# First two tiles of a fused induced attention and feed-forward kernel: second attention with tokens on the partitions, blocks in turns of four, weight loads spread among those of x

## The chip, the cores and the metric

One core of a Trainium2 chip runs the whole kernel. TensorE multiplies (PE in the rows; PEld is its weight loads), VectorE (DVE), ScalarE (ACT) and GpSimd (POOL) do the elementwise work, SyncE (SP) issues nearly all transfers. The metric is the device time of one execution in microseconds; lower is better.

## The reference

x is [4, 12480, 128] (4 batches of 12480 tokens), `inducing` is [32, 128], w_in [128, 2048], w_out [2048, 128]. The two weights come as 64-bit floats; everything else and the output are 32-bit.

```
def mab(q, kv):
    s = scale * (q @ kv.transpose(0, 2, 1))
    s = s - s.max(-1, keepdims=True)
    a = np.exp(s)
    a /= a.sum(-1, keepdims=True) + 1e-09
    return a @ kv
h = mab(I, x)            # first attention: 32 queries over 12480 tokens, per batch
y = mab(x, h)            # second attention: every token over the 32 rows of h
g = y @ w_in; g = np.maximum(0.01 * g, g)
out = g @ w_out
```

## The kernel before, in words

The second attention's weights A (32 per token) are never multiplied with h alone: h @ w_in is formed once per batch (`hws`, 2048 columns), so the feed-forward's first product is A @ (h @ w_in). The slope of 0.01 is taken out: the relu part carries 0.99, and a linear part A @ (h @ (0.01 w_in @ w_out)) is added at the end (`w12` is 0.01 w_in @ w_out, `m2s` is h @ w12). Values that feed the fast matmuls are split into a rounded part and a rest (hi and lo): A's halves lie stacked in four blocks of 32 partitions (hi, lo, hi, lo: tile `A4`), `hws` likewise, and w_out is `w_hi` and `w_lo`.

Tokens are taken in tiles of 512 columns; six groups of 2048 tokens (four tiles each) and a rest of 192 make up a batch. A tile is 16 slots, one per block of 128 columns of w_in. In slot u, `ffn_first` (L745) does one matmul into `ph` (L750), a relu on ScalarE into `ghi` (L758) and the rest on VectorE into `glo` (L760), three slots ahead; `ffn_second` (L770) does three matmuls into `po` (L778), and at a tile's last slot one more with `m2s` (L784). `store` transposes `po` on VectorE (L794) and writes it out. `ph` has three buffers, so the fourth first-product waits for the first `glo`.

All engines get their work in the order in which the program emits it; nothing is reordered but TensorE's weight loads. The main loop (L875 to L904) emits per slot the two feed-forward parts and then one step of each of several generators: conversions (`late`), weights, stores, stacking, second attentions, the next batch's first attention. A step marked HEAVY puts up a `debt` of 3, which holds back the other debt-bound generators for three slots.

Ahead of the loop is the ramp for batch 0. `first_batch` (L465) issues 25 transfers of x, with the four w_in chunks (512 KB each, one per 512 columns) behind the transfers named in LOADS (L69, counted from 0), and then works group by group: transposes of x on TensorE (L499), ScalarE copies (L502), scores against `inducing` (L268), running maximum and exponential (L280 to L329), sums h (L388). ROUNDS and DRAIN (L73, L77) say which background steps go between these: "l" is a quarter of the conversion of a weight chunk (`from_double`, L110: L123 and L124; L128; L132; L136 and two GpSimd steps L139, L140), "t" a turn of one w_in chunk by four transposes (L213). Five rounds convert one chunk each; the last round and the drain before hT (`normalise`, L452) convert the rest but one. w_out's chunks are split into `w_hi` (ScalarE, L188) and `w_lo` (GpSimd, L189), each one chunk behind its conversion.

Then, from hT on, RAMP (L78) interleaves `expand_weights` (hT @ w_in, four products L576, each split by ScalarE L555 and VectorE L557) with the second attention of group 0 (`second`, L624) on VectorE: scores L268, transpose L639, maximum L642, subtract L644, exponential L650, sum L654 to L656, multiply L658, transpose L667. `stack_first` (L708) spreads tile 0's A over the partitions with a matmul (L713), ScalarE (L716) and two VectorE steps (L719); tiles 1 to 3 of group 0 go by `stack` (L671) with 4 transfers each. The other groups' second attentions run in the loop with their two tensor steps on GpSimd (L644, L658 with POOL as engine). The w12 product (four groups of four matmuls, L225) is begun in the ramp and ended in the loop.

## Time and profile before

| what | us |
|---|---|
| median of 3 runs | 1626.44 (1625.77 to 1627.32) |
| the profiled execution | 1626.58 |
| its span | 1624.8 |
| TensorE busy | 1600.9 (99%) |
| VectorE busy | 1291.0 (79%) |
| ScalarE busy | 1008.7 (62%) |
| GpSimd busy | 109.4 (7%) |
| first feed-forward matmul starts | 62.32 |
| HBM read, written | 48.94 MB, 25.56 MB |

The span is what the trace covers, from the first instruction to the last; the execution's own time is 1.8 us longer. Busy is the time in which an engine ran an instruction. Matmuls are pipelined, so a busy TensorE is one that always has a next matmul. The rows below give durations of single instructions, what an engine waited for in square brackets, and the granted clock of TensorE (PEclk, 1.00 for 2.4 GHz and 0.50 for 1.2 GHz).

### The profile page before, as it was taken

The numbers are of one execution on the slowest core, as the hardware profiler recorded it, in microseconds if no ns is written. First come the engines' busy times: TensorE is split into PE (matmuls) and PEld (weight loads), VectorE is DVE, ScalarE is ACT, GpSimd is POOL, SyncE is SP. The second block draws the span as 40 slices with busy tenths as digits, with TensorE's granted clock in tenths as the row PEclk, the third lists the DMA queues.
The fourth block names the chain that finished last, engine by engine and source line by source line (L and its number), as shares of the span: only waits on it lengthen the run. The fifth ranks groups of instructions, "written<-read, shape, count | busy, mean of one in ns | idle before, by whom it ended". The sixth has DMA issues, their size and how long they took to land.

```text
span 1624.8 us, 22382 instructions
## 1 busy us (share of the span) xinstructions
PE 1600.9 (99%) x7881; PEld 1257.6 (77%) x7881; DVE 1291.0 (79%) x2228; ACT 1008.7 (62%) x1767; POOL 109.4 (7%) x108
## 2 busy tenths in 40 slices
PE   7799999999999999999999999999999999999998
PEld 5577777777778777777777777777777788888886
DVE  6788888787888887877787888877878777777776
ACT  5466666666666665666666666656666666666665
POOL 3310000000001000000010000000001000000000
PEclk9899999999999999999999999999999999999999
DMA  7323323522224344522123434532212111212211
GB/s 262 74 56 53 69 64 70 114 64 58 46 43 95 50 96 95 101 65 53 33 46 74 80 70 102 104 68 50 59 25 40 34 31 39 41 25 41 42 23 20
DMA packets 401503, 104.44 MB, mean 64 GB/s; under 512 B 372432, under 2 KB 374896, under 8 KB 401392
## 3 DMA queue, kind: packets, MB, share of 16 engines
q1 hardware_dynamic: 401344, 103.01, 31.3%
q8 instruction: 62, 1.02, 0.3%
q14 instruction: 49, 0.40, 0.1%
q10 hardware_dynamic: 48, 0.02, 0.0%
HBM read 48.94 MB, written 25.56 MB: 46 GB/s over the span
## 4 chain that ended last, share of the span: by engine, by line
PE 96%; DVE 2%; DMA 1%; ACT 0%; issue 0%; SPq 0%; DVEq 0%
PE po L778 67%; PE ph L750 23%; PE s_ps L268 3%; PE po L784 1%; PE h_ps L388 1%; DMA xr<-in_x_dram 1%; DVE cv_a L124 0%; PE xT_ps L499 0%; DVE cv_a L132 0%; PE mx_ps L297 0%; DVE glo L760 0%; DVE ay L416 0%; PE winT_ps L213 0%; ACT ghi L758 0%; PE w_ps L225 0%
## 5 line engine op out<-in xcount | busy, mean ns | idle before, releaser
L760 DVE SCALAR_TENSOR_TENSOR glo<-ph,ghi 128x512 fp32r<-128x512 f32 (+1 forms) x1568 | 1051.6, 681 | 303.9 <-ACT ghi L758 298.7
L758 ACT ACTIVATE ghi<-ph 128x512 fp32r<-128x512 f32 (+1 forms) x1568 | 933.6, 597 | 573.5 <-PE ph L750 571.8
L750 PE MATMUL ph<-A,hws 128*128 128x512 f32 (+1 forms) x1600 | 622.8, 393 | 3.1 <-DVE A L719 2.3
L778 PE MATMUL po<-ghi,w_hi 128*128 128x512 f32 (+1 forms) x1568 | 618.6, 395 | 0.0
L778 PE MATMUL po<-glo,w_hi 128*128 128x512 f32 (+1 forms) x1568 | 617.3, 394 | 0.0
L778 PE MATMUL po<-ghi,w_lo 128*128 128x512 f32 (+1 forms) x1568 | 613.8, 391 | 0.0
L750 PEld LDWEIGHTS ph<-A,hws 128*128 128x128 f32 x1600 | 300.7, 188 | 91.3 <-DVE glo L760 13.3
L778 PEld LDWEIGHTS po<-ghi,w_lo 128*128 128x128 f32 x1568 | 294.7, 188 | 70.1
L778 PEld LDWEIGHTS po<-glo,w_hi 128*128 128x128 f32 x1568 | 294.7, 188 | 66.5
L778 PEld LDWEIGHTS po<-ghi,w_hi 128*128 128x128 f32 x1568 | 294.8, 188 | 61.0
L689 POOL TENSOR_TENSOR alo<-aT,ahi 128x512 fp32r<-128x512 f32 x24 | 31.2, 1299 | 735.4 <-ACT ahi L684 590.5
L794 DVE STREAM_TRANSPOSE osb<-po 128x512 f32<-128x512 f32 (+1 forms) x98 | 68.9, 703 | 1.7 <-PE po L784 1.7
L644 POOL TENSOR_TENSOR y<-y,mx 128x512 f32<-128x512 f32 (+1 forms) x27 | 25.4, 940 | 419.9 <-DVE mx L642 419.9
L369 DVE STREAM_TRANSPOSE xT<-xc 128x512 f32<-128x512 f32 x72 | 50.5, 701 | 0.0
L658 POOL TENSOR_TENSOR y<-y,sm 128x512 f32<-128x512 f32 (+1 forms) x27 | 25.4, 939 | 212.9 <-DVE sm L656 130.2
L784 PE MATMUL po<-A,m2s 128*128 128x512 f32 (+1 forms) x100 | 38.6, 389 | 0.0
L388 PEld LDWEIGHTS h_ps<-xr,ay 128*32 128x32 f32 (+1 forms) x784 | 22.5, 112 | 12.6 <-issue 12.4
L268 PE MATMUL s_ps<-xT,indT 128*32 128x512 f32 x192 | 27.3, 642 | 1.6 <-ACT xT L502 1.6
L388 PE MATMUL h_ps<-xr,ay 128*32 128x128 f32 (+1 forms) x784 | 28.0, 280 | 0.0
L268 PE MATMUL s_ps<-xT,hT 128*32 128x512 f32 x192 | 25.6, 605 | 0.0
L280 DVE TENSOR_SCALAR_CACHE_REDUCE e<-s_ps 128x512 f32<-128x512 f32 (+1 forms) x28 | 17.1, 612 | 7.7 <-PE s_ps L268 7.2
L784 PEld LDWEIGHTS po<-A,m2s 128*128 128x128 f32 x100 | 18.7, 187 | 4.2
(98 smaller groups left out, 390.5 us busy)
## 6 DMA issues: line engine op xcount, KB each, us to landing
xr<-in_x_dram SPq DMA_DIRECT2D x96, 256.0 KB, 4.4
out_dram<-osb SPq DMA_DIRECT2D x384, 64.0 KB, 2.2
xc<-in_x_dram SPq DMA_DIRECT2D x288, 64.0 KB, 2.7
A<-ahi SPq DMA_DIRECT2D x190, 64.0 KB, 2.0
A<-alo SPq DMA_DIRECT2D x190, 64.0 KB, 2.0
raw<-in_moe_w_in_dram SPq DMA_DIRECT2D x4, 512.0 KB, 7.9
raw<-in_moe_w_out_dram SPq DMA_DIRECT2D x4, 512.0 KB, 6.6
hws<-hwhi SPq DMA_DIRECT2D x24, 64.0 KB, 2.0
```

Of the source, the lines that this page charges most:

```text
L268: nc.tensor.matmul(dst, lhsT, rhs, start=True, stop=True)
L369: nc.vector.transpose(t[:, j, :], blk.rearrange("p n c -> p (n c)"))
L388: nc.tensor.matmul(hp[32 * k : 32 * k + 32, :C], ay[:rows, 4 * q + k, :], xb[:rows, k, :], start=(q == 0), stop=(4 * q + 4 >= K), tile_pos ...
L644: eng.tensor_tensor(out=yv, in0=yv, in1=mx[:rows, :K].unsqueeze(2).broadcast_to([rows, K, M]), op=ALU.subtract,)
L658: eng.tensor_tensor(out=yv, in0=yv, in1=smv.unsqueeze(2).broadcast_to([rows, K, M]), op=ALU.mult)
L689: (eng or nc.gpsimd).tensor_tensor(out=alo[sl], in0=aT.pop((b, g))[: 32 * J, :], in1=ahi[sl].bitcast(F32), op=ALU.subtract,)
L750: nc.tensor.matmul(ph[:, o : o + w], hw[b][1][:, f * P : (f + 1) * P], A4[t][:, o : o + w], start=True, stop=True,)
L758: nc.scalar.activation(ghi[:, :n], ph[:, :n], AF.Relu)
L760: nc.vector.scalar_tensor_tensor(out=glo[:, :n], in0=ph[:, :n], scalar=0.0, in1=ghi[:, :n].bitcast(F32), op0=ALU.max, op1=ALU.subtract,)
L778: nc.tensor.matmul(po[:, :n], w[:, f, :], r[:, :n], start=(f == 0 and r is ghi and w is w_hi), stop=False)
L784: nc.tensor.matmul(po[:, o : o + w], hw[b][2], a4[:, o : o + w], start=False, stop=(o + w == n),)
L794: nc.vector.transpose(osb[:, :n], po[:, :n])
```

## The change

The x transfers that carry a weight chunk behind them are now the fifth, ninth, thirteenth, seventeenth and twenty-first (counted from 1), and the fifth chunk is w_out's first, in a buffer of its own. Two chunks of conversion (w_out's third and fourth) move into the loop, the second ends in the drain; the split of w_out is a generator of its own (`parts_of_w_out`), and w12 is summed chunk by chunk with a VectorE step each. Tiles 0 and 1 no longer go through `second` and the stacking: `quick` makes each tile's scores with the tokens on the partitions (x as the weights, hT's 32 columns as the moving operand), does maximum, exponential and sum along 32 columns on VectorE and ScalarE, and turns the result to the stacked layout by 16 matmuls with the identity. `stack_first` goes. Group 0's `second` now runs in the loop like the others, for tiles 2 and 3. Only the first of the four hT @ w_in products and its split are ahead of the loop. Slots of tiles 0 and 1 alternate in turns of four blocks (slots 0 to 3 tile 0, 4 to 7 tile 1, 8 to 11 tile 0, ...); from tile 2 on the order is as before. The values of batch 1 wait until weights and linear part of batch 0 are done.

```
-    LOADS = [3, 5, 7, 9]
+    LOADS = [4, 8, 12, 16, 20]
     ROUNDS = [
         [""] * 5, ["l", "l", "", "", "ll", "", ""], *[["l", "l", "", "", "ll", "", "", ""]] * 4,
-        ["ll", "ll", "", "", ""],
+        ["l", "", "l", "", ""],
     ]
-    DRAIN = ["", "", "llt", "t", "", "t", "", "", "tll"]
-    RAMP = ["wwm", "w", "w", "", "", "wl", "w", "", "", "w", "wll"]
+    DRAIN = ["", "", "s", "lt", "l", "", "t", "", ""]
+    QUICK = 2
+    TURN = 4
...
+        nc.vector.tensor_tensor(out=low_rows, in0=own[:, 1:2], in1=own[:, 3:4], op=ALU.add)
+        nc.vector.tensor_scalar(
+            out=signs, in0=low_rows, scalar1=2.0, scalar2=-1.0, op0=ALU.mult, op1=ALU.add
+        )
...
     def load_w_out(c):
-        raw = sb.tile([P, 4, P, 2], I32, tag="xc", name="raw", bufs=3)
+        tag, bufs = ("xc", 3) if c else ("hws", 2)
+        raw = sb.tile([P, 4, P, 2], I32, tag=tag, name="raw", bufs=bufs)
...
+    def parts_of_w_out():
+        for c in range(NF // 4):
+            while c >= len(ready):
+                yield
             if c:
-                split_w_out(c - 1)
-            yield
-        split_w_out(NF // 4 - 1)
-        yield
+                yield from idle(3)
+            split_w_out(c)
+            yield
...
     def setup_w12():
         for c in range(NF // 4):
-            while c == len(wraws) or (late and c == len(wraws) - 1):
+            while c >= len(ready):
                 yield
+            if c == len(ready) - 1:
+                yield from idle(3)
+            acc = aux_ps("w12_ps")
             for f in range(4):
                 nc.tensor.matmul(
-                    acc[:, :P], winTs[c][:, f, :], wraws[c][:, f, :],
-                    start=(c == 0 and f == 0), stop=(c == NF // 4 - 1 and f == 3),
+                    acc[:, :P], winTs[c][:, f, :], wraws[c][:, f, :], start=(f == 0), stop=(f == 3)
                 )
...
-                    xT[0, g] = sb.tile([P, K, J, 32], F32, tag="xT", name="xT", bufs=RING)
+                    shape = [P, K, J, 32] if g else [P, J, 32 * K]
+                    xT[0, g] = sb.tile(shape, F32, tag="xT", name="xT", bufs=RING)
...
         if b == 0:
...
             for c in range(4):
                 sl = slice(c * TOK, (c + 1) * TOK)
-                yield from split(hws[:, sl], pws[c], TOK, 1.0 - SLOPE)
+                pw = ps_s.tile([P, TOK], F32, tag="hp", name="hw_ps")
+                nc.tensor.matmul(pw, hT, w_in_sb[:, sl], start=True, stop=True)
                 yield
...
+                yield from split(hws[:, sl], pw, TOK, 1.0 - SLOPE)
+                yield
             return
...
+    def quick(t):
+        b, g, (j,) = tiles[t][0]
+        hT = hw[b][0]
+        sp = aux_ps("q_ps")
+        for c in range(4):
+            nc.tensor.matmul(
+                sp[:, c * M : (c + 1) * M], xT[b, g][:, j, c * P : (c + 1) * P], hT[:, :M],
+                start=True, stop=True,
+            )
+        yield
+        sv = sp[:, : 4 * M].rearrange("p (c m) -> p c m", m=M)
+        mx = sb.tile([P, 4], F32, tag="mx", name="qmx")
+        nc.vector.tensor_reduce(out=mx, in_=sv, op=ALU.max, axis=AX.X)
+        y = sb.tile([P, 4, M], F32, tag=("hwhi", "hwlo")[t], name="qy", bufs=1)
+        nc.vector.tensor_tensor(
+            out=y, in0=sv, in1=mx.unsqueeze(2).broadcast_to([P, 4, M]), op=ALU.subtract
+        )
+        nc.scalar.activation(y, y, AF.Exp, scale=SCALE)
+        yield
+        sm = sb.tile([P, 4], F32, tag="sm", name="qsm")
+        nc.vector.tensor_reduce(out=sm, in_=y, op=ALU.add, axis=AX.X)
+        nc.vector.tensor_scalar_add(sm, sm, 1e-9)
+        nc.vector.reciprocal(sm, sm)
+        nc.vector.tensor_tensor(
+            out=y, in0=y, in1=sm.unsqueeze(2).broadcast_to([P, 4, M]), op=ALU.mult
+        )
+        yield
+        pa = ps_o.tile([P, TOK], F32, tag="po", name="a4_ps")
+        for c in range(4):
+            for r in range(4):
+                nc.tensor.matmul(
+                    pa[32 * r : 32 * r + 32, c * P : (c + 1) * P], y[:, c, :], ident,
+                    start=True, stop=True, tile_position=(0, 32 * r),
+                )
+        yield
         A4[t] = a4 = sb.tile([P, TOK], F32R, tag="A4", name="A4", bufs=A4_BUFS)
...
+        nc.scalar.mul(a4, pa, signs)
+        yield
+        nc.vector.scalar_tensor_tensor(
+            out=a4, in0=pa, scalar=low_rows, in1=a4.bitcast(F32), op0=ALU.mult, op1=ALU.subtract
+        )
+        yield
...
+    slots = [
+        (t, f) for f0 in range(0, NF, TURN) for t in range(QUICK) for f in range(f0, f0 + TURN)
+    ]
+    slots += [(t, f) for t in range(QUICK, NT) for f in range(NF)]
...
+        one, two = [quick(0)], [quick(1)]
+        for lane in (
+            one, two, weights, one, two, turning, one, one, weights, one, two, two,
+            weights, one, two, two,
+        ):
+            step(lane)
+        stacks[0] = stacks[0][QUICK:]
         stacking = [stack(s) for s in stacks]
-        weights = [chain(*weights, *twelve, expand_linear(0))]
-        seconds = [second(0, g) for g in [1, 2, RG, 3, 4, 5]]
+        linear = [chain(*turning, *twelve, expand_linear(0))]
+        seconds = [second(0, g) for g in [0, 1, 2, RG, 3, 4, 5]]
...
             step(late)
+            step(splits)
             step(weights)
+            step(linear)
             if not debt[0]:
                 step(stores)
             step(stacking)
-            if not weights and not debt[0]:
+            if not debt[0]:
                 step(seconds)
...
-                if values:
+                if values and not ((linear or weights) and b == 0):
```

## Rows read from the trace of the kernel before

**Rows 1.** The chain of waits that ended last: its shares of the span by engine.
```profile
PE 96%; DVE 2%; DMA 1%; ACT 0%; issue 0%; SPq 0%; DVEq 0%
```
**Rows 2.** Busy time of each engine in four stretches: stretch, its length, busy us and instructions of each engine, granted clock, share of the transfer engines, GB/s.
```profile
0.00:62.30 62.30, 45.23 (x409) 29.61 (x410) 42.77 (x117) 31.37 (x66) 21.30 (x22) 0.94 0.58 183
62.30:68.60 6.30, 5.72 (x13) 4.09 (x14) 3.54 (x6) 4.19 (x8) 1.39 (x2) 0.53 0.69 117
68.60:101.00 32.40, 32.40 (x164) 26.11 (x163) 24.80 (x47) 19.39 (x35) 7.05 (x6) 1.00 0.33 76
101.00:1618.80 1517.80, 1517.58 (x7298) 1197.74 (x7296) 1219.18 (x2059) 953.79 (x1658) 79.64 (x79) 1.00 0.30 59
```
**Rows 3.** The chain of waits in order of time, pieces of the first two tiles: start us, us, what. L784 is a tile's last matmul; the one at 100.80 ends tile 1.
```profile
71.11 0.89 PE w_ps L225 x8
...
88.77 0.70 PE po L778 x3
89.47 0.23 PE ph L750
...
100.80 0.24 PE po L784
```
**Rows 4.** TensorE in order of time, the first groups of the first attention: transposes of x (L499) and scores (L268); in brackets what it waited for.
```profile
13.43 1.97 PE L499 MATMUL xT_ps<-ident,xr 128*128 128x128 f32 x8 [0.54 <-DMA xr<-in_x_dram]
...
16.07 1.93 PE L268 MATMUL s_ps<-xT,indT 128*32 128x512 f32 x8 [0.45 <-ACT xT L502]
...
22.06 1.04 PE L268 MATMUL s_ps<-xT,indT 128*32 128x512 f32 x8
23.04 1.97 PE L499 MATMUL xT_ps<-ident,xr 128*128 128x128 f32 x16
...
26.41 1.06 PE L268 MATMUL s_ps<-xT,indT 128*32 128x512 f32 x8 [0.28 <-ACT xT L502]
```
**Rows 5.** Busy time by stretch, 10 to 20 us; the columns are those of rows 2.
```profile
10.00:20.00 10.00, 9.01 (x44) 5.92 (x37) 5.30 (x16) 4.42 (x9) 2.55 (x2) 1.00 1.04 398
```
**Rows 6.** All engines in order of time, last round and drain: two conversion steps, the maximum's matmul, a w_in turn, the h product of group 5, the copy that makes hT.
```profile
39.98 0.68 DVE L132 SCALAR_TENSOR_TENSOR cv_a<-cv_a,cv_b 128x512 int32<-128x512 int32 x1
...
40.70 0.43 DVE L136 TENSOR_SCALAR cv_b<-cv_a 128x512 int32<-128x512 int32 x1
...
42.88 0.59 PE L297 MATMUL mx_ps<-rd,e 128*128 128x4 f32 x2 [2.87 <-DVE rd L292]
...
43.33 1.09 PE L213 MATMUL winT_ps<-ident,w_in_sb 128*128 128x128 f32 x4
...
44.35 1.94 PE L388 MATMUL h_ps<-xr,ay 128*32 128x128 f32 x32
...
50.30 0.27 ACT L461 COPY hT<-hT_ps 128x128 f32<-128x128 f32 x1 [0.58 <-PE hT_ps L459]
```
**Rows 7.** The same view between hT and the first feed-forward matmul.
```profile
53.23 1.79 DVE L644 TENSOR_TENSOR y<-y,mx 128x512 f32<-128x512 f32 x1
...
60.05 0.59 ACT L716 CAST A<-a_ps 128x512 fp32r<-128x512 f32 x1 [3.31 <-PE a_ps L713]
...
62.32 1.62 PE L750 MATMUL ph<-A,hws 128*128 128x512 f32 x3 [2.31 <-DVE A L719]
```
**Rows 8.** The same view, rows that serve as prices: a 128-column VectorE step out of PSUM, an h product at the upper clock level, two hT @ w_in products (four records).
```profile
22.49 0.28 DVE L402 COPY hacc<-h_ps 128x128 f32<-128x128 f32 x1
...
25.05 1.08 PE L388 MATMUL h_ps<-xr,ay 128*32 128x128 f32 x32
...
51.62 1.98 PE L576 MATMUL hw_ps<-w_in_sb,hT 128*128 128x512 f32 x4
```
**Rows 9.** The chain of waits, pieces of the first slots: start us, us, what.
```profile
63.75 0.70 DVE glo L760
...
66.57 0.43 PE ph L750
67.00 1.28 PE po L778 x3
```
**Rows 10.** Busy time by stretch of 2 us; the columns are those of rows 2, the granted clock is the third from the right.
```profile
40.00:42.00 2.00, 0.01 (x2) 0.00 (x0) 1.97 (x7) 1.51 (x4) 0.73 (x1) 0.74 0.03 4
...
46.00:48.00 2.00, 2.00 (x18) 1.71 (x10) 1.00 (x5) 0.59 (x1) 0.00 (x0) 0.56 0.06 8
...
60.00:62.00 2.00, 0.01 (x1) 0.00 (x0) 1.92 (x4) 0.59 (x1) 0.00 (x0) 0.86 0.18 28
```
**Rows 11.** All engines in order of time: conversion steps on VectorE with and without a GpSimd instruction under way, a ScalarE cast that waits for GpSimd, the attention's subtract on GpSimd.
```profile
38.04 1.27 POOL L140 TENSOR_TENSOR wraw<-cv_a,cv_t 128x512 f32<-128x512 f32 x1
...
38.37 1.22 DVE L124 TENSOR_SCALAR cv_a<-raw 128x512 f32<-128x512 f32 x1
...
44.09 1.50 DVE L128 TENSOR_SCALAR cv_b<-raw 128x512 int32<-128x512 int32 x1
...
55.78 0.43 DVE L124 TENSOR_SCALAR cv_a<-raw 128x512 f32<-128x512 f32 x1
...
69.83 0.62 ACT L188 CAST w_hi<-wraw 128x512 fp32r<-128x512 f32 x1 [1.89 <-POOL wraw L140]
...
86.86 1.05 POOL L644 TENSOR_TENSOR y<-y,mx 128x512 f32<-128x512 f32 x1 [13.31 <-DVE mx L642]
```
**Rows 12.** The tile that holds batch 1's to 3's rounded h @ w_in: instruction, count, durations in ns, first and last start in us.
```profile
L601 ACT ACTIVATE hwhi<-hw_ps x3: 592/592/592, 392.4 to 1129.4; 128x512 fp32r<-128x512 f32 x3
```

More of the change, by code (lines that the diff above doesn't have):

```diff
@@ L99, in induced_attention_then_leaky_ffn @@
     own = const.tile([P, 4], F32, tag="own", name="own")
+    low_rows = const.tile([P, 1], F32, tag="low_rows", name="low_rows")
+    signs = const.tile([P, 1], F32, tag="signs", name="signs")
     w_in_sb = const.tile([P, DFF], F32, tag="w_in_sb", name="w_in_sb")
@@ L263, in columns_product @@
         dst, rhs = ps[32 * j : 32 * j + 32, :w], xT[b, g]
-        if b == 0:
+        if b == 0 and g:
             dst, rhs = dst.rearrange("p (k r) -> p k r", r=32), rhs[:, :, j, :]
@@ L478, in first_batch @@
             if i in LOADS:
-                raws.append(load_w_in(LOADS.index(i)))
+                c = LOADS.index(i)
+                raws.append(load_w_in(c) if c < NF // 4 else load_w_out(0))
         chains, ays = {}, {}
@@ L501, in turn @@
                 )
+            t = xT[0, g]
+            if g == 0:
+                t = t.rearrange("p j (k r) -> p k j r", r=32)
             nc.scalar.copy(
-                xT[0, g][:, 4 * q : 4 * q + nk].rearrange("p k j r -> p (k j r)"),
-                pt[:, : nk * rows],
+                t[:, 4 * q : 4 * q + nk],
+                pt[:, : nk * rows].rearrange("p (k j r) -> p k j r", k=nk, r=32),
             )
@@ L567, in expand_weights @@
         if b == 0:
-            pws = []
-            def product():
-                c = len(pws)
-                if c == 1:
-                    pw = ps_s.tile([P, TOK], F32, tag="hp", name="hw_ps")
-                else:
-                    pw = aux_ps("hw_ps")
-                nc.tensor.matmul(
-                    pw, hT, w_in_sb[:, c * TOK : (c + 1) * TOK], start=True, stop=True
-                )
-                pws.append(pw)
-            for _ in range(3):
-                product()
-                yield
             for c in range(4):
                 sl = slice(c * TOK, (c + 1) * TOK)
-                yield from split(hws[:, sl], pws[c], TOK, 1.0 - SLOPE)
+                pw = ps_s.tile([P, TOK], F32, tag="hp", name="hw_ps")
+                nc.tensor.matmul(pw, hT, w_in_sb[:, sl], start=True, stop=True)
                 yield
-                if c == 0:
-                    product()
-                    yield
+                yield from split(hws[:, sl], pw, TOK, 1.0 - SLOPE)
+                yield
             return
@@ L706, in stack @@
                 yield
-    def stack_first(t):
-        b, g, _ = tiles[t][0]
+    def quick(t):
[33 more added lines that the diff above has]
+        yield
         A4[t] = a4 = sb.tile([P, TOK], F32R, tag="A4", name="A4", bufs=A4_BUFS)
-        pa = gen_ps("a4_ps")
-        nc.tensor.matmul(
-            pa, e128[:M].rearrange("p j m -> p (j m)"), aT[b, g][:M, :], start=True, stop=True
+        nc.scalar.mul(a4, pa, signs)
+        yield
+        nc.vector.scalar_tensor_tensor(
+            out=a4, in0=pa, scalar=low_rows, in1=a4.bitcast(F32), op0=ALU.mult, op1=ALU.subtract
         )
-        nc.scalar.copy(a4, pa)
         yield
-        for o in (32, 96):
-            nc.vector.tensor_tensor(
-                out=a4[o : o + 32], in0=pa[o : o + 32], in1=a4[o : o + 32].bitcast(F32),
-                op=ALU.subtract,
-            )
     tiles = []
@@ L770, in ffn_second @@
     def ffn_second(u):
-        t, f = divmod(u, NF)
+        t, f = slots[u]
         parts, n = spans(t)
@@ L851, in induced_attention_then_leaky_ffn @@
         late = [chain(setup_w_in(), setup_w_out())]
-        turning, twelve = [turn_w_in()], [setup_w12()]
-        lanes = {"t": turning, "l": late, "m": twelve}
+        turning, splits, twelve = [turn_w_in()], [parts_of_w_out()], [setup_w12()]
+        lanes = {"t": turning, "l": late, "s": splits}
         for todo in first_batch():
@@ L856, in induced_attention_then_leaky_ffn @@
                 step(lanes[lane])
-        lanes["w"] = weights = [expand_weights(0)]
-        for _, todo in zip(second(0, 0, nc.vector), RAMP):
-            for lane in todo:
-                step(lanes[lane])
-        first = stack_first(0)
-        next(first)
-        for lane in RAMP[-1]:
-            step(lanes[lane])
-        drain(first)
-        stacks[0].pop(0)
+        weights = [expand_weights(0)]
+        one, two = [quick(0)], [quick(1)]
[5 more added lines that the diff above has]
+        stacks[0] = stacks[0][QUICK:]
         stacking = [stack(s) for s in stacks]
-        weights = [chain(*weights, *twelve, expand_linear(0))]
-        seconds = [second(0, g) for g in [1, 2, RG, 3, 4, 5]]
+        linear = [chain(*turning, *twelve, expand_linear(0))]
+        seconds = [second(0, g) for g in [0, 1, 2, RG, 3, 4, 5]]
         stores, scores, values = [], [], []
@@ L875, in induced_attention_then_leaky_ffn @@
         for u in range(NT * NF):
-            t, f = divmod(u, NF)
+            t, f = slots[u]
             if f == 0 and tiles[t][0][1:] == (0, [0]):
```

16 lines of the change are left out of this document (9 added, 7 removed).

## The prediction

> **What bounds the kernel now.** I read the chain of waits first, then busy time by stretch, then the ramp's timelines. The chain that ended last is TensorE for 96% [rows 1]. By stretch [rows 2], TensorE is full from 101.0 us to 1618.8 (1517.6 of 1517.8 us); it is short of work only in the first 62.3 us (45.2 busy) and slow for the next 6 (granted clock 0.53, near the 1.2 GHz level). A slot (one first-product matmul, three second-product matmuls) is 0.23 + 0.70 = 0.93 us [rows 3], and 1568 of them are the span. So the change, which touches the ramp and the first 32 slots, is worth the difference in when slot 31 is done: 101.03 us here [rows 3]. Later work only shifts: batch 1 has its weights at 392.4 us [rows 12], and its first tile comes 384 slots after the start, near 62 + 384 x 0.99 = 442 us ((1618.8 - 62.3)/1568 a slot), so the few slots by which its loads and sums now begin later have some 50 us of cover; without it each slot late would cost 0.93.
>
> The profiled execution took 1626.58 us (span 1624.8), 0.14 above the median of the runs; the sum is made against it.
>
> **Part 1, loads spread.** Group 1's third quarter arrived at 13.43, after TensorE had waited 0.54 us for it, since 12.89 [rows 4]. Two weight chunks lay ahead of it, now one: 0.5 MB less at 398 GB/s [rows 5] is 1.3 us, so it is there at 12.1 and the 0.54 us gap closes. Four weight chunks lay ahead of group 2, now two. The last group gets two quarters' worth (0.5 MB, 1.3 us) more ahead of it, and I cost that at nothing: its transposes come after five rounds of work; if that cover went, up to 1.3 us. Beyond the gap, the level of TensorE's clock matters: eight transposes take 1.97 us at 13.43, sixteen take 1.97 at 23.04 [rows 4]; the granted-clock column reads 1.00 in both, so it says nothing before 40 us. TensorE went to 2.4 GHz while it worked without a gap after 16.07. The change gives it unbroken work from 9.05. Bounds: no earlier rise, 0.5 us; a rise before the third quarter, 3.1. I take a rise by the second group's scores, the nearest row being the unbroken stretch after 16.07: scores at 15.5, 1.04 long, then the 3.37 us from transposes to the next scores (23.04 to 26.41 [rows 4]) = 19.9, against 22.06. **2.2 us earlier.** Later rounds keep their length, since VectorE's queue sets it. Two small steps in the setup cost nothing (VectorE waits there for TensorE's first product); group 0's copies now write in runs of 32 columns, as many columns as before: I take nothing, with 0.6, one copy more on the path, as the other end.
>
> **Part 2, the drain.** One conversion chunk is half moved out of the last round: VectorE loses L132 and L136 there (0.68 and 0.43), but ScalarE's exponential must still follow the maximum, so I give 0.5. One w_in turn (1.09) is no longer ahead of the last big h product [rows 6]; a conversion step of 0.68 lands between h's accumulation and the sums. Net 0.8. hT at 50.57 [rows 6] becomes 50.57 - 2.2 - 1.3 = 47.1. Bounds: 0.3 if the inserted step delays the sums in full, 2.2 if the shorter wait keeps TensorE at 2.4 GHz (h 1.08, as in [rows 8], and not 1.94).
>
> **Part 3, from hT to the first feed-forward matmul.** Before: 62.32 - 50.57 = 11.75 us [rows 6, 7], with full-width VectorE steps, one of 1.79. After, along tile 0's path: four score matmuls (8 records with 128-column weights; nearest row, the w12 group, 0.89 [rows 3]) 0.95; maximum and subtract on 128 columns, 0.28 each [rows 8], 0.65; exponential 0.35; sum, add, reciprocal, multiply 1.2, with tile 1's maximum and subtract ahead of them in the queue (0.4 more); sixteen matmuls onto the partitions, as the 32-record h group, 1.08 [rows 8]; ScalarE 0.59 [rows 7]; the hws split ahead of the last VectorE step, and that step, 0.68 each less what overlaps, 1.0; hops 0.15. Sum 6.35. Beside it TensorE does tile 1's scores, one hw product (half of 1.98) and one w_in turn. **5.4 us gained**; all three parts: 2.2 + 1.3 + 5.4 = 8.9, the first matmul at 53.4. If TensorE is at 1.2 GHz here, scores and transposition cost about 1.5 more.
>
> **Part 4, work moved behind the start.** Three hw products at 0.99 (1.98 for two [rows 8]: 2.97), one w_in turn 0.49, group 0's second scores 1.0, a fourth w12 group 0.89 [rows 3, 4]: **5.4 us more for TensorE** among the first 32 slots. Before, 62.32 to 101.03 is 38.7 us, of which 32 x 0.93 + 2 x 0.24 + 3 x 0.23 + 3 x 0.89 + 1.4 (scores and small ones) = 35.1 is work; 3.6 went on the first fill and on the low level ([rows 9]: 1.28 for 0.70).
>
> **Part 5, new waits in the first slots.** Two conversions (8 VectorE, 4 GpSimd steps), three w_out splits and group 0's attention now stand in the loop. I lay the queues out in emission order, counting from the first matmul. (a) Fill: the fourth matmul waits for the first glo, 1.1. (b) The third hw product needs the buffer that VectorE frees in slot 2's split. TensorE's fourth first-product starts at 1.8, then 0.93, hw product 1.0, turn 0.45 and scores 1.0 make 5.2; the next first-product (0.45) and relu (0.6) let VectorE start slot 1's glo at 6.25. It has glo, L128, a transpose, glo, L132, split: 0.68 + 0.42 + 0.72 + 0.68 + 0.68 + 0.69 to 10.1 ([rows 6, 9, 11] and their like); TensorE, from 5.2 with w12 0.89 and three slots, is there at 8.9: 1.2. (c) The fourth likewise: the third ends at 11.1; VectorE has from 12.15 glo 0.68, L124 1.2 beside GpSimd work [rows 11], a maximum 0.69, glo 0.68, L128 0.42, split 0.69, to 16.5; TensorE, three slots and w12, is there at 14.8: 1.7. (d) Slot 9's exponential waits for a GpSimd subtract queued behind conversion and split, 3 x 1.27 + 1.05 [rows 11] after L136 ends at 19.6, so 24.5; the exponential (0.6), ScalarE's next relu (0.6) and glo (0.68) stand behind it, to 26.3; TensorE, from 17.5 with six slots and w12, needs that glo at 24.0: 2.3. Such a block is in the trace: ScalarE stood 1.89 for w_out's sum with a relu behind it [rows 11]. Sum 6.3 against 3.6: **2.7 lost.** All this is at 2.4 GHz: TensorE has nearly unbroken work from hT on, where before it had little from 57 to 62 and the level had fallen by 62 [rows 10]. Four A transfers per tile come at slots 18 and 19 and are needed at slots 29 and 45; ahead of them on SyncE are only the block loads, the third set waiting for slot 5's L128, so I cost them at nothing; if they came late, a slot each.
>
> On (c): the rows show L124 at 1.22 when it begins inside a GpSimd instruction, 0.43 when not [rows 11]. The Trainium skill (SBUF — State Buffer, "Two separate sides") says that VectorE and GpSimd hold a port pair exclusively for a whole instruction, and the loser waits. By that, L124 and then L128 can each lose to a GpSimd instruction, one more 1.3 on the fourth product: the time would be 1626.9. The trace agrees that VectorE's step is the one that waits (L128 took 1.50 when it began inside a split [rows 11]), but in the order laid out above L128 begins just after GpSimd is done.
>
> **Sum.** -8.9 + 5.4 + 2.7 = -0.8 us: 1625.8 on the profiled run's scale, **1625.6** on the median's.
>
> **Rivals.** 0.2% (3.25 us) is about what a measurement of this kernel can tell from no change.
> 1. *The waits do not come* (faster). If VectorE and GpSimd run ahead of TensorE in the first ten slots, (b), (c) and (d) shrink and their 5.2 us stay gained: down to 1620.4; two thirds of them, 1622.1. For it: TensorE's inserted 5.4 us give VectorE time, about 14 us of work each over slots 0 to 8. Against: the emission order, VectorE's in-order queue. It decides once (b) to (d) together fall below about 2.7.
> 2. *TensorE at 1.2 GHz from hT through the first slots* (slower). Scores and transposition 1.5 more, then hw product, turn and scores at double time 2.5, the first two slots 0.8 each ([rows 9]: 1.71 for 0.93), less 1.1 that falls into wait (b): +4.5, hence 1630.1. For it: the level had fallen by 42 and came back only at about 47.8, and fell again at 61 [rows 10]; waits (b) to (d) leave TensorE idle. Against: from hT on it has work nearly without gap, which it had not before. It decides once the low level lasts about 4 us.
> 3. *The spread loads do nothing* (no change): TensorE stays at 1.2 GHz until the same point and only the 0.54 gap closes: 1.7 us less gained, 1627.3.
> 4. *VectorE waits for two GpSimd instructions* (no change): L124 and L128 each begin inside one, as L124 did at 38.37 and L128 at 44.09 [rows 11]; the fourth hw product is 1.3 later: 1626.9. The Trainium skill's port rule (SBUF — State Buffer, "Two separate sides") is this case.
>
> **How the numbers follow.** Forecast 0.28, rival 3 0.13, rival 4 0.12: together 0.53 within 0.2%. Rival 1: 0.31, faster by over 0.2%. Rival 2: 0.16, slower by over 0.2%. Range: downwards the forecast less most of rival 1 (4.6 of 5.2), 1621.0; upwards nearly to rival 2, 1630.0; part 1's bounds (-0.9, +1.7) and part 2's (-0.9, +1.0) lie inside.
>
> **What would show it.** First matmul L750 between 52 and 55 us; scores of group 2 near 19.9, not 21.5 (part 1); hT near 47.1; from hT to that matmul 6 to 7 us; the third and fourth hw products waiting for a VectorE split by 1 to 2 us each; ScalarE idle 2 us or more before the attention's exponential, released by GpSimd; slot 31 done near 100.3; after it no waits. Wrong if the start comes after 56, if the granted clock is low after it, if TensorE's waits in the first 16 slots sum to under 3 us, or if waits appear beyond slot 32 (A transfers late).

## The result, and the profile after

The changed kernel takes **1634.83 us** (median of 4, 1633.72 to 1636.24) against 1626.66 for the kernel before beside it: ratio 1.0051 (95% interval 1.0034 to 1.0068), 8.2 us slower. The forecast was 1625.6, its range ended at 1630.0: wrong. The profiled execution took 1636.24 us (span 1634.2), 1.4 above its median.

Busy time in four stretches, with the columns of [rows 2], cut near the first feed-forward matmul (59.56) and near the end of slot 31 (its last matmul starts at 108.53 and ends at 108.92):

```profile
0.00:59.50 59.50, 44.51 (x461) 31.70 (x461) 35.29 (x114) 29.27 (x63) 17.63 (x19) 0.86 0.55 181
59.50:68.60 9.10, 8.09 (x41) 5.26 (x41) 6.04 (x12) 5.77 (x12) 0.00 (x0) 1.00 0.01 2
68.60:108.70 40.10, 34.83 (x159) 26.66 (x159) 29.85 (x55) 20.40 (x38) 13.51 (x11) 0.96 0.34 59
108.70:1628.00 1519.30, 1518.03 (x7300) 1197.77 (x7299) 1220.45 (x2064) 953.14 (x1659) 80.52 (x80) 1.00 0.30 60
```

The ramp (all that is ahead of the first feed-forward matmul) is 2.8 us shorter, not 8.9; its granted clock fell from 0.94 to 0.86. The first slots start at the upper level (1.00 where [rows 2] has 0.53), but from 68.6 to 108.7 TensorE is idle for 5.3 us, where before it had no gap. Behind slot 31 only 1.3 us are idle.

TensorE, first groups (transposes L522, scores L289), against [rows 4]:

```profile
8.93 1.12 PE L522 MATMUL xT_ps<-ident,xr 128*128 128x128 f32 x4 [1.56 <-DMA xr<-in_x_dram]
10.72 1.93 PE L289 MATMUL s_ps<-xT,indT 128*32 128x512 f32 x8 [0.68 <-ACT xT L528]
16.90 1.07 PE L289 MATMUL s_ps<-xT,indT 128*32 128x512 f32 x8 [0.56 <-ACT xT L528]
21.27 1.06 PE L289 MATMUL s_ps<-xT,indT 128*32 128x512 f32 x8 [0.27 <-ACT xT L528]
```

The second group's scores run at the upper level (1.07, not 1.93), as forecast, but the fourth quarter of x is late: TensorE waits 1.56 us for it, the first scores come at 10.72 (before: 9.05), and the third group's at 21.27, not 19.9.

All engines, drain to first feed-forward matmul, against [rows 6, 7]:

```profile
38.08 0.38 PE L318 MATMUL mx_ps<-rd,e 128*128 128x4 f32 x2 [2.06 <-DVE rd L313]
41.95 0.59 PE L318 MATMUL mx_ps<-rd,e 128*128 128x4 f32 x2 [2.37 <-DVE rd L313]
42.47 1.94 PE L409 MATMUL h_ps<-xr,ay 128*32 128x128 f32 x32
44.05 1.28 POOL L199 TENSOR_TENSOR w_lo<-wraw,w_hi 128x512 fp32r<-128x512 f32 x1 [5.18 <-ACT w_hi L198]
44.74 1.14 DVE L136 SCALAR_TENSOR_TENSOR cv_a<-cv_a,cv_b 128x512 int32<-128x512 int32 x1
48.41 0.58 ACT L231 COPY winT<-winT_ps 128x512 f32<-128x512 f32 x1 [2.34 <-PE winT_ps L229]
48.90 0.40 ACT L477 ACTIVATE hs<-hacc,rz 128x128 f32<-128x128 f32 x1
50.19 0.27 ACT L482 COPY hT<-hT_ps 128x128 f32<-128x128 f32 x1 [0.89 <-PE hT_ps L480]
50.50 3.62 PE L724 MATMUL q_ps<-hT,xT 128*128 128x32 f32 x16 [0.35 <-ACT hT L482]
53.94 2.05 PE L597 MATMUL hw_ps<-w_in_sb,hT 128*128 128x512 f32 x2
55.78 1.06 PE L229 MATMUL winT_ps<-ident,w_in_sb 128*128 128x128 f32 x4
59.56 0.73 PE L792 MATMUL ph<-A,hws 128*128 128x512 f32 x2 [0.73 <-DVE A L757]
```

Busy time by 2 us, against [rows 10] (granted clock third from the right):

```profile
40.00:42.00 2.00, 0.05 (x1) 0.05 (x1) 1.59 (x8) 0.33 (x2) 0.00 (x0) 0.50 0.03 4
46.00:48.00 2.00, 1.79 (x10) 1.40 (x10) 1.43 (x7) 0.07 (x1) 1.33 (x2) 0.50 0.11 18
52.00:54.00 2.00, 2.00 (x11) 2.00 (x11) 0.58 (x2) 0.31 (x1) 0.00 (x0) 0.50 0.00 0
56.00:58.00 2.00, 2.00 (x46) 1.65 (x48) 0.58 (x3) 1.09 (x2) 0.00 (x0) 0.74 0.00 0
88.00:90.00 2.00, 2.00 (x8) 1.63 (x7) 1.97 (x5) 0.19 (x1) 1.11 (x2) 0.50 0.00 0
```

The waits for two maxima leave TensorE idle for 2.06 and 2.37 us, from 36 and from 39.6 on; the clock goes to the 1.2 GHz level and stays there to 57, through work without a gap from 50.5 on. In the kernel before it fell there too and was back near 47.8. So both tiles' scores take 3.62 us, and from hT to the first feed-forward matmul it takes 9.1 us where the forecast had 6.35.

All engines, first slots, and then TensorE's waits there (us in total, times, longest):

```profile
70.04 1.10 PE L597 MATMUL hw_ps<-w_in_sb,hT 128*128 128x512 f32 x2 [1.22 <-DVE hws L583]
76.42 1.10 PE L597 MATMUL hw_ps<-w_in_sb,hT 128*128 128x512 f32 x2 [1.61 <-DVE hws L583]
83.45 1.05 POOL L654 TENSOR_TENSOR y<-y,mx 128x512 f32<-128x512 f32 x1
84.53 0.63 ACT L660 ACTIVATE y<-y 128x512 f32<-128x512 f32 x1 [4.16 <-POOL y L654]
86.42 0.50 PE L792 MATMUL ph<-A,hws 128*128 128x512 f32 x1 [2.44 <-DVE glo L802]
87.46 1.64 PE L243 MATMUL w_ps<-wraw,winT 128*128 128x128 f32 x8
```
```profile
PE ph L792 <- DVE glo L802: 3.4, 2, 2.4
PE hw_ps L597 <- DVE hws L583: 2.8, 2, 1.6
PE po L820 <- DVE osb L836: 1.0, 1, 1.0
```

These are waits (a) to (d) of the forecast, at its sizes, and one it lacks: tile 2's first second product waits 1.0 us for the PSUM buffer of tile 0, whose store transpose (L836) ends at 109.96.

### The profile page after: what moved, and what is told of

The parts are those of the page before. It is cut to its first block, busy times and chain, and to the rows that moved or that the text cites. A ratio compares the mean times of both kernels' runs of the same rounds, so it can differ in the third digit from the quotient of the medians.

```text
span 1634.2 us, 22558 instructions
## 1 busy us (share of the span) xinstructions
PE 1605.8 (98%) x7959; PEld 1261.4 (77%) x7959; DVE 1292.3 (79%) x2243; ACT 1008.6 (62%) x1770; POOL 111.7 (7%) x110
## 3 DMA queue, kind: packets, MB, share of 16 engines
HBM read 48.94 MB, written 25.56 MB: 46 GB/s over the span
## 4 chain that ended last, share of the span: by engine, by line
PE 95%; DVE 2%; DMA 1%; ACT 1%; POOL 0%; issue 0%; SPq 0%; DVEq 0%
PE po L820 66%; PE ph L792 23%; PE s_ps L289 3%; PE po L826 1%; PE h_ps L409 1%; DMA xr<-in_x_dram 1%; DMA raw<-in_moe_w_in_dram 0%; DVE cv_a L128 0%; DVE glo L802 0%; ACT ghi L800 0%; PE hw_ps L597 0%; PE mx_ps L318 0%; PE q_ps L724 0%; DVE cv_a L136 0%; DVE ay L437 0%
## 5 line engine op out<-in xcount | busy, mean ns | idle before, releaser
L836 DVE STREAM_TRANSPOSE osb<-po 128x512 f32<-128x512 f32 (+1 forms) x98 | 68.9, 703 | 1.7 <-PE po L826 1.7
L390 DVE STREAM_TRANSPOSE xT<-xc 128x512 f32<-128x512 f32 x72 | 50.5, 701 | 0.0
L289 PE MATMUL s_ps<-xT,indT 128*32 128x512 f32 x192 | 26.4, 623 | 1.7 <-ACT xT L528 1.7
L289 PE MATMUL s_ps<-xT,hT 128*32 128x512 f32 x192 | 25.6, 605 | 0.0
```

What stands on the lines that cost most here:

```text
L289: nc.tensor.matmul(dst, lhsT, rhs, start=True, stop=True)
L390: nc.vector.transpose(t[:, j, :], blk.rearrange("p n c -> p (n c)"))
L836: nc.vector.transpose(osb[:, :n], po[:, :n])
```

## The experiments

The spans of all profiles, split at the first feed-forward matmul (us; "max" is the start of the last maximum's product; the w_in column says behind which quarter of x the first load goes):

| kernel | w_in | first scores | max to first matmul | first matmul | rest of span | median | ratio to before (95%) |
|---|---|---|---|---|---|---|---|
| before | 4th | 9.05 | 19.4 | 62.32 | 1562.5 | 1626.66 | |
| changed | 5th | 10.72 | 17.6 | 59.56 | 1574.6 | 1634.83 | 1.0051 (1.0034 to 1.0068) |
| e1_loads_after | 4th | 8.85 | 18.2 | 57.06 | 1574.1 | 1633.28 | 1.0044 (1.0032 to 1.0057) |
| e2_loads_alone | 5th | 9.51 | 19.4 | 60.66 | 1562.4 | 1625.19 | 0.9996 (0.9988 to 1.0005) |
| e3_vector | 5th | 9.55 | 16.5 | 56.58 | 1570.2 | 1629.21 | 1.0021 (1.0011 to 1.0031) |
| e4_two_buffers | 5th | 10.02 | 16.4 | 56.97 | 1574.5 | 1633.92 | 1.0051 (1.0037 to 1.0065) |
| f1_waits | 5th | 10.19 | 16.4 | 57.11 | 1569.1 | 1630.04 | 1.0020 (1.0011 to 1.0029) |
| f2_filled | 5th | 9.11 | 14.1 | 55.57 | 1570.2 | 1629.01 | 1.0017 (1.0008 to 1.0026) |
| f3_drain | 5th | 10.72 | 17.0 | 58.99 | 1570.5 | 1630.84 | 1.0023 (1.0014 to 1.0033) |
| g1_fitted | 5th | 10.47 | 12.2 | 53.12 | 1569.8 | 1624.37 | 0.9991 (0.9982 to 1.0000) |
| g2_fitted_buffers | 5th | 9.74 | 12.2 | 52.63 | 1581.3 | 1637.90 | 1.0069 (1.0056 to 1.0082) |
| g3_before_filled | 5th | 10.44 | 18.2 | 59.41 | 1561.9 | 1622.23 | 0.9978 (0.9969 to 0.9988) |
| g4_fitted_loads | 4th | 8.49 | 12.2 | 52.10 | 1582.2 | 1637.06 | 1.0065 (1.0051 to 1.0079) |
| h1_clock_alone | 5th | 11.12 | 14.3 | 56.47 | 1574.6 | 1632.57 | 1.0040 (1.0026 to 1.0053) |
| h2_third_product | 5th | 10.56 | 12.2 | 54.03 | 1568.5 | 1624.12 | 0.9988 (0.9979 to 0.9997) |
| h3_filled_loads | 4th | 10.78 | 18.3 | 60.27 | 1561.9 | 1622.35 | 0.9978 (0.9969 to 0.9987) |

The experiments were run in rounds, each with the kernel before beside it, whose median went from 1625.60 to 1626.66; rows of different rounds (e, f, g, h) are compared by the ratio. Spans are those of one profiled execution per kernel, and its ramp varies: the changed kernel, e3, e4 and f1 have the same ramp, and their first feed-forward matmul starts at 59.56, 56.58, 56.97 and 57.11.

**e1, the first load's place**, on the changed kernel:
```
-    LOADS = [4, 8, 12, 16, 20]
+    LOADS = [3, 8, 12, 16, 20]
```


> The changed kernel with one number altered: the first w_in load goes behind the fourth quarter of x again, as in the kernel before, the others stay spread (behind the 9th, 13th, 17th and 21st). Theory A (the fourth quarter came 1.7 us late because a fifth quarter was issued ahead of the w_in load): first scores back from 10.72 to about 9.05 us, hT earlier by 0.5 to 1.5 us, time about 1633.8. Rival B (VectorE's rounds set the pace behind the first group, whatever arrives when): first scores earlier, but the sixth group's and hT within 0.3 us of the changed kernel's 34.66 and 50.2, time 1634.8. Rival C (the late quarter has to do with the total of loads, not with their order): first scores stay at 10.7.

First scores at 8.85, first matmul 2.5 us earlier, median 1.5 less (1.1 by the ratios, whose intervals overlap). It looked like theory A; see h3.

**e2, the loads alone**, on the kernel before:
```
-    LOADS = [3, 5, 7, 9]
+    LOADS = [4, 8, 12, 16]
```


> The kernel before with the four w_in loads spread as in the changed kernel (behind the 5th, 9th, 13th and 17th quarter), nothing else. My forecast on record for this part: third group's scores from 22.06 to 19.9 us and 2.2 us off the time, 1624.4. Theory A (what the changed kernel's trace shows): first scores later, at 10.7, third group's at 21.3, and by the sixth group 0.5 us of the gain left: time 1626.1, not to be told from 1626.6. Rival: the level of TensorE's clock in the drain comes out differently by a shift of this size, and the time moves by up to 2 us either way with the loads themselves worth 0.5.

Third group's scores at 20.10 (forecast 19.9, before 22.06), the second group's at the upper level (1.07); by the first matmul 1.66 us are left, in the medians 1.1, and the interval of the ratio still holds no change. Part 1's mechanism held in the trace, in its bounds; theory A has the third group's scores too late. The time (1625.2) lies between the forecast's 1624.4 and theory A's 1626.1.

**e3, group 0's attention on VectorE**, on the changed kernel:
```
-        seconds = [second(0, g) for g in [0, 1, 2, RG, 3, 4, 5]]
+        seconds = [second(0, g, None if g else nc.vector) for g in [0, 1, 2, RG, 3, 4, 5]]
```


> The changed kernel, with the two elementwise steps of group 0's second attention (subtract the maximum, multiply by the reciprocal) on VectorE instead of GpSimd. Theory A: ScalarE's exponential no longer stands behind a GpSimd instruction that ends at 84.50, so TensorE's wait of 2.44 us at 86.4 goes and with it the fall of the granted clock from 88 to 91 (about 2 us more): time 1634.8 - 4.4 = 1630.4. Rival B: VectorE has no room in these slots for two passes over 128x512 (0.7 us each by its other instructions), glo comes late instead, and 1 to 2 us remain: about 1632.5. Rival C: the clock falls anyway, since it follows the many short waits before it: only the wait goes, 1632.4.

Theory A: the rest of the span is 4.4 us shorter, the clock stays at 1.00 from 56 on, and only (a), (b), (c) and the store's wait are left. (The median, 1629.2, is a further 1.2 below theory A's 1630.4.)

```profile
PE hw_ps L597 <- DVE hws L583: 2.8, 2, 1.6
PE po L820 <- DVE osb L836: 1.0, 1, 1.0
PE ph L792 <- DVE glo L802: 0.9, 1, 0.9
```

**e4, a second buffer for the products**, on the changed kernel:
```
+                if c % 2:
+                    pw = aux_ps("hw_ps")
+                else:
+                    pw = ps_s.tile([P, TOK], F32, tag="hp", name="hw_ps")
```


> The changed kernel, with the second and fourth hw product in a buffer of another ring, so that a product no longer waits for the split of the one before it. Theory A: TensorE's waits of 1.22 and 1.61 us in front of the third and fourth product go: 1634.8 - 2.8 = 1632.0. Rival B: the split of each product takes as long as before and stands in ScalarE's and VectorE's queues ahead of the blocks' ghi and glo, so that half of the wait comes back in front of a first matmul of a block: 1633.4. Rival C: by moving the slots against ScalarE's exponential the wait of 2.44 us at 86.4 grows by what was won: 1634.8.

Rival C: the waits for the products went, and TensorE met the block behind the exponential that much sooner; a new wait of 1.7 us came for the ring of the scores.

```profile
PE ph L795 <- DVE glo L805: 4.5, 2, 3.6
PE w_ps L243 <- DVE y L652: 1.7, 1, 1.7
```

**f1, both and an earlier store transpose**, e3 with e4's edit and:
```
                 stores.append(store(t))
+                if t == 0:
+                    next(stores[0])
+                    next(stores[0])
```


> On the version with group 0's second attention on VectorE (1629.2): the second and fourth hw product in another ring, and tile 0's store transpose issued right behind its last block. Theory A: the three waits of TensorE that are left behind the start go, 1.2 + 1.6 in front of the third and fourth product and 1.0 in front of tile 2's first second product: 1629.2 - 3.8 = 1625.4, the first version below the kernel before. Rival B: with the products in the ring of the scores and of w12, a wait appears there (1.7 us was seen for it), so that only the store's 1.0 and about 1 of 2.8 are won: 1627.2. Rival C: TensorE's waits come back as waits for glo, since VectorE is what all of them wait for: 1629.

The store's wait is gone and w12's 1.7 is there again: rival B in kind. The rest of the span gained 1.1 us over e3; the median did not (1630.04 against 1629.21, ranges of over 3 us that overlap), and by the time alone it is none of the three.

**f2, work in the gaps**, on e3:
```
+    def fill():
+        for n in (14, 16, 5, 6, 8, 3):
+            pt = gen_ps("k_ps")
+            for _ in range(n):
+                nc.tensor.matmul(pt[:, :P], ident, ident, start=True, stop=True)
+            yield
```


> On the same version: 52 products of the identity with itself, whose results nobody reads, issued on TensorE in the gaps of the last rounds and of the drain (14, 16, 5, 6, 8 and 3 of them), nothing taken out. Theory A (the start comes 3 us later than I forecast because TensorE's clock stands at the lower level between the drain and the first feed-forward matmul): the granted clock stays at 1.0 from 34 us on, the last whole group's products take 1.08 us and not 1.94, the scores of the two tiles 1.9 and not 3.6, from hT to the first feed-forward matmul 6.3 us and not 9.1: time 1629.2 - 3.6 = 1625.6. Rival B (VectorE, ScalarE and the exponentials set that stretch, TensorE's rate is hidden): the clock rises and hT to the first feed-forward matmul stays over 8.5: 1629. Rival C: the added products push the real ones back and the clock falls all the same: 1630 to 1631.

The products stand in the last round and the drain. The clock stayed at 1.00, and from the scores to the first matmul it took 6.2 us, not 9.1: theory A for that stretch. The time did not follow (1629.0, nearest to rival B's 1629): a product costs 0.24 us, so 14 of them took 3.3 us in a gap of 2, and the last round grew from 3.96 us in e3 to 5.00.

**f3, the drain**, on e3:
```
-    DRAIN = ["", "", "s", "lt", "l", "", "t", "", ""]
+    DRAIN = ["", "", "", "l", "l", "", "", "", "s"]
```


> On the same version: out of the drain go the two transposes of w_in (they run among the first blocks instead) and the split of w_out's first part moves to the drain's end. Theory A (in the drain ScalarE's copy of the turned w_in stands ahead of hs and GpSimd's subtract holds up VectorE's conversion, as the changed kernel's trace shows): from the last maximum's product to hT 7 us and not 8, hT 1 us earlier; but 1.0 us of TensorE's work moves behind the start: time 1629.2, within 0.5. Rival B: TensorE has less to do in the drain, its clock stays low for longer, and the stretch from hT on is slower by up to 1 us: 1630. Rival C: hT is set by the chain of VectorE's small steps and nothing is won there: 1630.2.

At the same low clock, max to hT's copy is 48.94 - 41.98 = 7.0 us, not 8.2, and VectorE's L136 takes 0.68:

```profile
44.77 0.68 DVE L136 SCALAR_TENSOR_TENSOR cv_a<-cv_a,cv_b 128x512 int32<-128x512 int32 x1
...
47.65 0.40 ACT L477 ACTIVATE hs<-hacc,rz 128x128 f32<-128x128 f32 x1 [4.15 <-DVE hacc L429]
48.94 0.27 ACT L482 COPY hT<-hT_ps 128x128 f32<-128x128 f32 x1 [0.89 <-PE hT_ps L480]
```

So theory A for the drain. No gain came of it: the clock rises at about 57 here as in the changed kernel, so that from hT on it takes 9.8 us and not 9.1, and the median, 1630.8, is not below e3's. Rival B (fewer bursts in the drain keep the clock low) is nearer by its time, 1630, but is not shown: the changed kernel's clock was as low with all of them.

**g1, the fill cut to the gaps**: e3, f1's store, f3's drain, and f2 with (7, 8, 4, 4, 1).

> The changed kernel with group 0's second attention on VectorE, the transposes of w_in out of the drain, tile 0's store transpose issued right behind its last block, and added products of the identity sized to the gaps (7, 8, 4, 4 and 1, at 0.24 us each by the run with 52 of them, which had overfilled its gaps by about 1 us each). Theory A (what is lost at the start is TensorE's lower clock): granted clock 1.0 throughout, the last rounds as far apart as without the products, from hT to the first feed-forward matmul 6.2 us, from the last maximum's product to hT's use 6.5: time 1629.2 - 2.9 - 1.5 - 1.0 = 1623.8. Rival B (the chain of VectorE's small steps hides the rate of the clock in the drain, and only the stretch behind hT gains): 1625.3. Rival C (so few products don't hold the clock): 1627.

Theory A by its mechanism: the clock is at 1.00 throughout. The time, 1624.4, lies between its 1623.8 and rival B's 1625.3, and its interval still touches the kernel before.

```profile
40.95 0.39 PE L325 MATMUL mx_ps<-rd,e 128*128 128x4 f32 x2 [0.40 <-DVE rd L320]
41.27 1.08 PE L416 MATMUL h_ps<-xr,ay 128*32 128x128 f32 x32
...
46.52 0.27 ACT L489 COPY hT<-hT_ps 128x128 f32<-128x128 f32 x1 [0.58 <-PE hT_ps L487]
46.83 1.97 PE L731 MATMUL q_ps<-hT,xT 128*128 128x32 f32 x16
...
48.64 1.10 PE L604 MATMUL hw_ps<-w_in_sb,hT 128*128 128x512 f32 x2
...
49.58 0.60 PE L236 MATMUL winT_ps<-ident,w_in_sb 128*128 128x128 f32 x4
...
53.12 0.96 PE L799 MATMUL ph<-A,hws 128*128 128x512 f32 x3 [0.66 <-DVE A L764]
```
```profile
40.00:42.00 2.00, 1.60 (x35) 1.39 (x38) 0.96 (x9) 0.36 (x2) 0.00 (x0) 1.00 0.06 8
...
52.00:54.00 2.00, 1.34 (x23) 0.68 (x11) 1.55 (x3) 1.31 (x3) 0.00 (x0) 1.00 0.00 0
```

The h product takes 1.08 and the scores 1.97; hT's copy ends at 46.79 and the first matmul starts at 53.12, 6.33 us later: part 3's term (6.35) at the upper level. That hT itself comes near the forecast's 47.1 is luck: the last maximum is 0.75 later than forecast (40.95 against 40.2), and the drain, which here has f3's order too, 1.1 shorter (5.84 against 6.9).

**g2, g1 with e4's buffers and the attention begun at slot 6**:
```
-            if not debt[0]:
-                step(seconds)
+            if not debt[0] and u >= 6:
+                step(seconds)
```


> The same with the second and fourth hw product in the other ring, and group 0's second attention begun six slots later, so that its scores do not hold that ring when w12's products want it. Theory A: TensorE's waits of 1.2 and 1.6 us in front of the products go and none of 1.7 takes their place: 2.8 us under the version without it. Rival B: a wait of the blocks for glo comes instead, since each product's split is another 0.7 us of VectorE: 1 to 1.5 us under it.

Neither theory: the products' waits went, and the later tiles' A, which that attention feeds through DMA, came late; the clock fell in the hole.

```profile
PE ph L802 <- DMA A<-alo: 10.8, 2, 7.7
```

**g3, the kernel before with e2's loads and a fill** of (7, 10, 4, 7, 8), the last two in front of and behind the copies of tile 0's A.

> The kernel before with the w_in loads spread (1625.2) and products of the identity in its own gaps (7 and 10 in front of the last two maxima, 4 in front of hT, 7 in front of the copies of the first tile, 8 behind them), nothing else. Theory A (the lower clock in the drain and in the first slots costs the kernel before as well): its first three feed-forward matmuls 0.96 us and not 1.62, its first slots 0.93 us and not 1.3 to 1.9, together 2 to 3 us: 1622.7. Rival B: the gaps at the lower clock are ended by VectorE and the cost is hidden: 1625.

Theory A, the fastest here with h3: first matmuls 0.94 against 1.62 in [rows 7], first slots without the low level, and the drain 6.50 us where it took 7.69.

```profile
59.41 0.94 PE L757 MATMUL ph<-A,hws 128*128 128x512 f32 x3 [0.33 <-DVE A L726]
61.29 0.50 PE L757 MATMUL ph<-A,hws 128*128 128x512 f32 x1 [0.94 <-DVE glo L767]
62.32 0.40 PE L757 MATMUL ph<-A,hws 128*128 128x512 f32 x1
```

**g4, g2 with the first load behind the 4th quarter.**

> The version with the products in two rings, and the first w_in load behind the fourth quarter of x as in the kernel before. Theory A (the order of the loads lets the fourth quarter land late): first scores at 8.9 us and 0.5 to 1 us off the time of the version without it. Rival B (the landing of the first quarters varies from run to run, whatever the order): times within 0.3.

First scores 8.49, first matmul 0.5 us earlier, median 0.8 less in ranges that overlap: as theory A, weakly.

**h1, the clock alone**: the changed kernel with a fill of (7, 8, 4, 3, 1) and nothing else.

> The changed kernel with products of the identity in the gaps of the last rounds and of the drain (7, 8, 4, 3 and 1) and nothing else altered. Theory A (the lower clock from the drain to the first feed-forward matmul is what the start lost): from hT's copy to the first feed-forward matmul 6.3 us and not 9.1, the drain about 1 us shorter; 4 us off the 1634.8, 1630.8. Rival B (in the drain of the changed kernel ScalarE's copy and GpSimd's subtract set the pace, not TensorE): only the stretch behind hT gains, 1632. Rival C: the waits behind the start grow by what the start won, 1634.

2.3 us off the median (1.8 by the ratios). Max to first matmul is 3.3 us shorter than in the changed kernel: the drain takes 6.54 us and not 8.51, from hT on 7.73 and not 9.10. That would be more, but the clock fell once more at 50 to 54 (0.57), behind an idle stretch of a microsecond in front of hT, where VectorE's steps stood beside GpSimd's. The rest of the span did not move. The time, 1632.6, is nearest to rival B's 1632, but not for rival B's reason: the drain, with its order of work unchanged, gained more than the stretch behind hT, so TensorE's rate sets its pace in part.

**h2, g1 with the third product alone in the other ring** (e4's edit with c == 2).

> The version that took 1624.4, with the third hw product alone in the other ring; the second attention starts where it did. Theory A: the waits of 0.94 us in front of the third and the fourth product go, and nothing waits for the ring: 1624.4 - 1.9 = 1622.5. Rival B: the ring is wanted by the scores and w12 in the same slots and one wait of about 1 us comes: 1623.5. Rival C: a wait of the blocks for glo takes the place of both: 1624.4.

Theory A in the trace: no wait for a product or for the ring is left, and the rest of the span fell by 1.3 us. The median fell by 0.25 only, inside the ranges, which is rival C's time (1624.4).

```profile
PE ph L802 <- DVE glo L812: 1.3, 2, 0.9
PE ph L802 <- DVE A L767: 0.7, 1, 0.7
PE m_ps L638 <- DVE w L256: 0.2, 1, 0.2
```

**h3, g3 with the first load behind the 4th quarter.**

> The filled kernel of before (1622.2) with the first w_in load behind the fourth quarter of x, the others spread as they were. Here the clock stays at its upper level from 15 us on, so that a shift of the start goes through to the end. Theory A (the order lets the fourth quarter come late): first scores at 8.6 to 9 us and not 10.4, the sixth group's 0.5 to 1 us earlier, time 1621.5. Rival B (the landing varies from run to run and the order has no part in it): time 1622.2, within 0.4.

Rival B: first scores at 10.78 in the old order too, and the same time as g3 (1622.35 against 1622.23). Over all profiles they came at 8.49 to 10.78 in the old order (4 profiles) and 9.11 to 11.12 in the new (12). Three of the four in the old order are earlier than all twelve in the new, so an effect of the order is not ruled out; what decides the landing stays open.

## Why the prediction was wrong

By its own steps, on the profiled spans: forecast -0.8, measured +9.4, so 10.2 us to place (about 1 of them belongs to this execution: the medians differ by 8.2).

- **The start: forecast -8.9, measured -2.8; 6.1 of the miss.** To the last maximum 1.75 (40.2 forecast, 41.95): the late fourth quarter in the main, 1.7 at the first scores. The eleven other profiles with the new order of loads have the third group's scores at 18.4 to 21.5, in the middle 20.2, against 19.9 forecast and 21.27 here: part 1 is sound, and about 1 us of this term is this execution's landing.
- **Part 2 failed, 1.6** (max to hT 6.9 forecast, 8.5 measured, 7.7 before: outside its bounds). Two things share this. One is the order of work: I set the conversion step at 0.68, but L136 began inside GpSimd's split of w_out (44.05) and took 1.14, and the copy of the second w_in turn stands ahead of hs (h divided by its sums) on ScalarE (48.41, hs 48.90, its input ready at 48.04). The kernel before had such a split in its drain too, beside L128 (44.09, 1.50 us [rows 11]), but VectorE still waited 0.77 us for the h product behind it. The other is the clock, which before was back in the drain and here was not. At the low clock f3's order takes off 1.3 us (7.23); at the upper clock the changed kernel's own order takes 6.54 (h1), f3's 5.84 (g1). So the order is worth 1.3 or 0.7 and the clock 2.0 or 1.4, by which is taken away first. The Trainium skill (SBUF — State Buffer, "Two separate sides") names the collision: a VectorE step with two SBUF inputs and a GpSimd step that reads SBUF exclude each other. The trace agrees (1.14 against 0.68); I had applied the rule to the slots and not to the drain.
- **Part 3 failed, 2.75** (6.35 forecast, 9.10). The failing sentence (it stands in part 5) is that all this is at 2.4 GHz because TensorE has nearly unbroken work from hT on. It has, and the clock was still at 0.50 up to 57: it had fallen in the gaps at 36 and 40, and the drain's short bursts did not bring it back. In e3, e4 and f1 it was back between 44 and 48 (0.83 to 1.00 there) and fell again just before hT: 9.07 to 9.18 us all the same. I had written 1.5 for this into part 3 and rival 2; scores, product and turn at double time are 3.62 + 2.05 + 1.06 against 1.97 + 1.10 + 0.60 in g1, 3.1. With the gaps filled the term is 6.33.
- **Part 4 held.** With the waits out (h2) the rest of the span is 6.6 longer than that of the kernel before with its clock held (g3, h3), of which the drain's two turns, which h2 has moved too, are about 0.8 (the three turns among g1's slots take 0.52, 0.35 and 0.35 from their start to the next product's): 5.8 against 5.4. The small waits that are left (1.5 us in h2, 1.9 in g3) are not taken out.
- **Part 5 held wait by wait**: (a) 1.1 forecast, 0.95 measured; (b) 1.2, 1.22; (c) 1.7, 1.61; (d) 2.3, 2.44, and e3 shows (d)'s cause. But the sum lacked what (d) does to the clock: 0.50 from 88 to 90, and 87.46 to 91.14 for work that takes 2.07 at the upper level (0.89 + 0.93 + 0.25), 1.6 us. e1, where the clock did not fall, was only 0.5 us shorter over the first 32 slots: waits of 0.48 for glo and 0.19 for w12's sum came in its place. Up to slot 32 the miss is 2.5, the fall's 1.6 and 0.9 that I cannot place.
- **"After slot 31 no waits" failed, 1.5**: 1.0 for tile 0's store transpose. In turns of four, tile 0 ends four blocks before tile 1, and tile 2 wants its PSUM buffer four slots later, not sixteen. f1 and g1 show it; 0.5 is not placed.

Of the rivals, number 2 had the sign and half the mechanism (the low level from hT on), but the slots themselves ran at 1.00 up to wait (d). Rivals 1 and 3 are refuted by the waits' sizes and by e2; 4 did not occur (wait (c) is 1.61, without its 1.3 more).

What stays when the waits and the low clock are taken out: from the last maximum to the first matmul the change saves 6.1 us (18.3 to 12.2, g3 and h2; 5.4 of them behind hT, 11.74 to 6.34, as part 3 had it, and 0.7 by f3's order in the drain) and puts 6.6 behind it. With the clock held on both sides, the kernel before stands at 1622.2 and the changed one, with h2's other changes, at 1624.1. The change moves TensorE's work from ahead of the start to behind it, and on a span that TensorE bounds that gains nothing; the waits of (b) to (d) and of the store, the clock and the drain's order made the rest of the 8 us.

## What to carry to other kernels

Work that is moved out of a ramp into a loop which its engine bounds is paid in full there, so count the ramp's idle time that it closes, and only that. Price a ramp's TensorE work at the level of the clock that its own last gaps leave, not at the one that the unbroken work to come suggests; where the gaps were filled with products nobody reads, sized to them, both kernels gained (3.0 us for the kernel before, e2 to g3; about 2 for the changed one, h1). Delaying a chain that feeds a DMA needs its whole way to the consumer counted: in g2 six slots' delay cost 10.8 us of waits.

## What was not expected

- TensorE went on at 0.50 for 6 us of gapless work (50.5 to about 57), where in the kernel before the clock rose in the drain at about 47.8; and behind one idle stretch of 2.4 us at the upper level (83.98 to 86.42) it was low from 87.9 to 91.1, as it was in h1 behind 2.46 us, while in e1 the like stretch (2.44) did not lower it.
- The fourth quarter of x let the first scores start anywhere between 8.49 and 11.12 us in 16 profiles, in either order of the loads.
- A 128 x 128 fp32 product costs 0.24 us on TensorE in a row of them (14 in 3.32 us), two records each.
